# One sum, reciprocal and widening per unit in a top-k attention kernel with a maxout layer

## The chip, the cores and the metric

The kernel runs on one core of a Trainium2 chip. The metric is the device time of one execution in microseconds (us), as the median of three runs. One further execution was recorded by the hardware profiler; all rows below come from it. In the rows PE is the engine of the matrix products, PEld its weight loads, DVE the vector engine, ACT the engine that applies functions, POOL the general one, SP the one that issues transfers.

## What is computed

Attention over 8 batches of 8 heads, 576 positions of 64 values each, where each query keeps its 32 largest scores. The result goes through three products whose element-wise maximum is taken, and one output product.

```python
def _attn_ref(q, k, v):
    scores = scale * np.matmul(q, k.transpose(0, 1, 3, 2))
    kth = np.partition(scores, -top_k, axis=-1)[..., -top_k:-top_k + 1]
    scores = np.where(scores >= kth, scores, -1000000000.0)
    scores = scores - np.max(scores, axis=-1, keepdims=True)
    attn = np.exp(scores)
    attn = attn / (np.sum(attn, axis=-1, keepdims=True) + 1e-09)
    return np.matmul(attn, v)

def _moe_ref(x, w1, w2, w3, w_out):
    h = np.maximum(np.maximum(x @ w1, x @ w2), x @ w3)
    return h @ w_out
```

## The kernel before

**Units and groups.** Attention is cut into 80 units. 64 of them take two groups of 128 queries of one pair of heads, 16 are half units with one group (the last 64 queries of two pairs of heads). A group has two tiles of 128 rows by 576 scores, one for each head; `ssb` holds the scores.

**The steps of a unit.** `qk` (line 458, PE) makes the scores and `evac` (501, ACT) moves them out. `sweep` (510, DVE) takes maxima of seven parts of each row; `negate` and `pivot` (516 to 542) make of them a first guess at the 32nd largest. `sign` (550, ACT), `window` (555, POOL), `below` (559, DVE) and `pick` (570 to 575) find the exact value, and `mask` (598, DVE) pushes out the scores under it. `expo` (607, ACT) takes the exponential and the row sums. Then, group by group, `denominator` (615, ACT) adds 1e-9 to the two sums, `inverse` (622, DVE) takes the reciprocals, and `widen` (627, ACT) spreads the reciprocal of each head over 64 columns as `rsw`. `turn` (PE) transposes: pieces T(g,0) and T(g,1) are four 128x128 blocks each of the group's two tiles (658), and T(g,2) is one more block of the scores (653) and the widened reciprocals (655). `turned` (666, ACT) copies each of the three out of PSUM to `pT`. `values` (683, PE) multiplies by v; `scaled_x` (700, DVE) multiplies by the reciprocals; `high_x` (703, ACT) and `low_x` (707, POOL) split the result into two halves of 16 bits.

**The layer behind it.** The three products (`layer`, 740, PE), the maximum (747 on ACT, 749 on DVE), the split (752 on ACT, 755 on POOL) and the output product (`layer2`, 801, PE; 807 on ACT) are called the fill. A batch has a first part of 256 positions and a second of 320, and a part may start when the units of its positions are done. The weights come as raw words that DVE decodes (263 to 265), and ACT (309, 312) and POOL (315) cut into two halves, all inside the first 220 us: casts 1 to 18 at line 312 belong to the first products, six for each third of the columns, casts 19 to 24 to the output product.

**What sets the order.** Every step is a `Piece` with an engine, a cost and a rank: the number of its unit plus a shift from the table `OFFSETS`. `in_order` goes through a planned time and gives each engine its pieces one after the other; fill pieces go in between when nothing of higher rank can start. On PE a piece of qk is in mode "rows", one of `values` in "columns", all else in none; `STICK` says how much later a piece of the present mode may be and still be taken. The result is one fixed order for each engine; on the chip each engine goes through its own and waits where an operand isn't there yet. `rings` holds the number of buffers for each tile.

Of the kernel before, what the change touches and what calls it, by code (L numbers as in the profile page):

```python
# [33 lines left out]
AHEAD_OF_FILL = 6  # L34
STICK = 220.8
WINDOW = 150
# [105 lines left out]
PACE = 0.9  # L142
SAVED_IN = 2600.0
FIRST = ((0, 1),)
# [6 lines left out]
SCORES = 960  # L151
PATIENCE = {'PE': 137.2, 'DVE': 138.1, 'ACT': 0.0, 'POOL': 1.4, 'SP': 0.0}


@with_exitstack
def kernel(ctx, tc, q, k, v, moe_w1, moe_w2, moe_w3, moe_w_out, out):
    nc = tc.nc
# [139 lines left out]
    def cut(j, part):  # L297
# [16 lines left out]
        def low():  # L314
# [4 lines left out]
    rings = {nm: Ring(k) for nm, k in dict(s=2, tr=2, m=2, ssb=NSSB, L=NSM, nA=NSM, n8=NSM, nb=3, w=NWB, oh=2, pm=PMB, rs=3, sums=3, den=3,  # L319
                                           rsw=2, pT=1, xs=2, junk=2, early=2, stage=2, books=2, vt=6, x=2, h1=3, ob=2, ws=2, qk=3).items()}  # L320

# [114 lines left out]
    def open_unit(n):  # L436
        b, hps, us = units[n]
        if b not in books:
            books[b] = (wk.tile([P, NT, NW], F32, name="Q"), wk.tile([P, NT], F32, name="kth"), wk.tile([P, NT], F32, name="lost"))
        nt = tiles_of(n)  # L440
        i0 = hps[0] * 2 * NU + 2 * us[0] if us[0] < NU else NP * 2 * NU + hps[0]
        Q, kth, lost = books[b]
        st[n] = dict(nt=nt, ssb=[], s={}, w={}, rsw={}, Q=Q[:, i0:i0 + nt], kth=kth[:, i0:i0 + nt], lost=lost[:, i0:i0 + nt])

# [172 lines left out]
    def inverse(n, g):  # L617
        d = st[n]
        if g == 0:
            d["rs"] = sm.tile([P, 4], F32, name="rs", bufs=3)  # L620
        ts = slice(2 * g, 2 * g + 2)
        nc.vector.reciprocal(d["rs"][:, ts], d["den"][:, ts])
# [36 lines left out]

    def turned(n, g, i):  # L660
        d = st[n]
        if (g, i) == (0, 0):
            d["pT"] = wk.tile([P, 2, 10, P], F32, name="pT", bufs=1)
        pt, pT = d.pop(("pt", g, i)), d["pT"][:, g].rearrange("p i n -> p (i n)")
        m = 512 if i < 2 else 2 * P
        nc.scalar.copy(pT[:, 512 * i:512 * i + m] if i < 2 else pT[:, 8 * P:10 * P], pt[:, :m])  # L666

    def values(n):
# [5 lines left out]
        for x, hp in enumerate(hps):  # L674
            vt = v_of[b, hp]
            for i in range(5):
                for h in range(2):
                    block = 4 * h + i if i < 4 else 8
                    if us[0] < NU:
                        to, keys = xp[64 * h:64 * h + 64, :P * len(us)], d["pT"][:, 0:len(us), block, :]  # L680
                    else:
                        to, keys = xp[64 * h:64 * h + 64, 64 * x:64 * x + 64], d["pT"][:, 0, block, 64 * x:64 * x + 64]
                    nc.tensor.matmul(to, vt[:, block if i < 4 else 8 + h, :], keys, start=(i == 0), stop=(i == 4))  # L683
# [11 lines left out]
    def scaled_x(n):  # L695
        b, hps, us = units[n]
        d = st[n]
        xs = d["xs"] = sm.tile([P, 2 * P], F32, name="xs", bufs=2)
        x, xp = (t[:, :P * len(us)].rearrange("p (t n) -> p t n", n=P) for t in (xs, d["xp"]))
        nc.vector.scalar_tensor_tensor(x, xp, vs_of[b][0], d["pT"][:, 0:len(us), 9, :], ALU.mult, ALU.mult)  # L700

# [170 lines left out]
    def attention(n):  # L872
# [61 lines left out]
        last_x[:] = [d["x", nt - 1]]  # L934
        held(n, "nb").extend(d["x", t] for t in range(nt))
        for g in gs:
            xs = [d["x", 2 * g], d["x", 2 * g + 1]]
            p(("d", g), "ACT", 130, lambda g=g: denominator(n, g), needs=xs + ([d["d", 0]] if g else []), takes=[] if g else [("den", held(n, "den"))])
            p(("r", g), "DVE", 72, lambda g=g: inverse(n, g), needs=[d["d", g]] + ([d["r", 0]] if g else []), takes=[] if g else [("rs", held(n, "rs"))])
            p(("z", g), "ACT", 280, lambda g=g: widen(n, g), needs=[d["r", g]], takes=[("rsw", held(n, "rsw", g))])  # L940
            held(n, "den").append(d["r", g])
            held(n, "sums").append(d["d", g])
            held(n, "rs").append(d["z", g])
            for i in range(3):
                rel = []
                p(("T", g, i), "PE", 470 if i < 2 else 240, lambda g=g, i=i: turn(n, g, i),
                  needs=[xs[i]] + last_v if i < 2 else [*xs, d["z", g], *last_v], takes=[("tr", rel)])
                p(("E", g, i), "ACT", 478 if i < 2 else 264, lambda g=g, i=i: turned(n, g, i),
                  needs=[d["T", g, i]] + ([] if (g, i) == (0, 0) else [d["E", 0, 0]]), takes=[("pT", held(n, "pT"))] if (g, i) == (0, 0) else [])
                rel.append(d["E", g, i])  # L950
                held(n, "pm", g).append(d["T", g, i])
            held(n, "rsw", g).append(d["T", g, 2])
        m = len(us) * P
# [131 lines left out]
    with tc.If(redo != 0):  # L1085
        with tc.For_i(0, B, 1) as b:
# [6 lines left out]
            for A in range(0, NP, 2):  # L1093
                for hp in (A, A + 1):
                    load_qk(B, hp)
                for x in [(B, (hp,), (u,)) for hp in (A, A + 1) for u in range(NU)] + [(B, (A, A + 1), (NU,))]:
# [6 lines left out]
                    for t in range(2):  # L1103
                        mask(i, t)
                        expo(i, t)
                    denominator(i, 0)
                    inverse(i, 0)
                    widen(i, 0)
                    for t in range(3):
# [56 lines left out]
```

## Time and profile before

| | |
|---|---|
| median of 3 runs | 1206.98 us (1206.4 to 1207.8) |
| profiled execution, own time | 1208.61 us |
| profiled execution, span from first to last instruction | 1206.8 us |
| busy share of the span: PE, DVE, ACT, POOL | 93%, 90%, 85%, 46% |
| mean granted clock of PE | 0.961 of full speed |
| chain that ended last: PE, DVE, ACT, POOL | 54%, 17%, 6%, 2% of the span |

The busy share is an average over three stages. In the first some 200 us PE works with gaps and at a clock that is granted in part, while the weights are decoded beside the first units. From there to about 1110 us PE and DVE are both nearly always busy. In the last 90 us DVE and ACT fall off and PE goes on alone. Matmuls are pipelined and their ends are modelled, so a PE that the page shows as busy may still be held up between two of them.

### The profile page before, as it was taken

The numbers are of one execution on the slowest core, as the hardware profiler recorded it, in microseconds if no ns is written. First come the engines' busy times: TensorE is split into PE (matmuls) and PEld (weight loads), VectorE is DVE, ScalarE is ACT, GpSimd is POOL, SyncE is SP. The second block draws the span as 40 slices with busy tenths as digits, with TensorE's granted clock in tenths as the row PEclk, the third lists the DMA queues.
The fourth block names the chain that finished last, engine by engine and source line by source line (L and its number), as shares of the span: only waits on it lengthen the run. The fifth ranks groups of instructions, "written<-read, shape, count | busy, mean of one in ns | idle before, by whom it ended". The sixth has DMA issues, their size and how long they took to land.

```text
span 1206.8 us, 27344 instructions
## 1 busy us (share of the span) xinstructions
PE 1126.2 (93%) x8799; PEld 775.9 (64%) x8799; DVE 1087.3 (90%) x5376; ACT 1025.1 (85%) x2701; POOL 549.4 (46%) x503
## 2 busy tenths in 40 slices
PE   6458678999999999999999999999999999999997
PEld 3225545666776658667676758666676767666865
DVE  7999989999999989999999999999999999999310
ACT  6799899999979999898888989989989898897411
POOL 2353446555454455454543544445445444546110
PEclk8679768999999999999999999999999999999999
DMA  7244501101310102020301102020100101000000
GB/s 265 75 168 151 200 1 64 38 16 48 128 32 30 51 19 71 10 71 16 114 32 43 39 18 72 18 63 2 56 26 30 51 19 30 10 11 1 19 18 29
DMA packets 28631, 65.00 MB, mean 54 GB/s; under 512 B 3009, under 2 KB 3265, under 8 KB 28481
## 3 DMA queue, kind: packets, MB, share of 16 engines
q1 hardware_dynamic: 28176, 62.76, 15.5%
q8 instruction: 71, 1.16, 0.4%
q14 instruction: 80, 0.65, 0.2%
q10 hardware_dynamic: 304, 0.43, 0.1%
HBM read 49.02 MB, written 14.16 MB: 52 GB/s over the span
## 4 chain that ended last, share of the span: by engine, by line
PE 54%; DVE 17%; ACT 6%; POOL 2%; issue 2%; POOLq 0%; ACTq 0%; DVEq 0%
PE m L740 24%; PE m L801 8%; PE tr L683 7%; PE tr L658 7%; PE s L458 6%; DVE ssb L598 5%; DVE L L510 4%; DVE Q L559 3%; ACT pm L607 2%; POOL w L555 2%; ACT w L550 2%; DVE h L749 1%; ACT pT L666 1%; PE tr L653 1%; DVE nR L534 1%
## 5 line engine op out<-in xcount | busy, mean ns | idle before, releaser
L555 POOL TENSOR_TENSOR w<-ssb,w 128x576 f32<-128x576 f32 x288 | 402.2, 1416 | 280.3 <-ACT w L550 225.4
L740 PE MATMUL m<-xh,wall 128*128 128x256 f16 (+1 forms) x2304 | 435.2, 287 | 4.6 <-POOL wall L315 2.4
L740 PEld LDWEIGHTS <-wall 128*128 128x128 f16 x3456 | 336.8, 98 | 91.1 <-issue 10.5
L740 PE MATMUL m<-xl,wall 128*128 128x320 f16 (+1 forms) x1152 | 330.1, 287 | 0.0
L510 DVE MAX8 L<-ssb 128x8 f32<-128x82 f32 (+1 forms) x2016 | 312.5, 229 | 6.0 <-ACT ssb L501 6.0
L607 ACT ACTIVATE pm<-ssb,nb 128x576 f32<-128x576 f32 x288 | 223.3, 776 | 45.3 <-DVE ssb L598 44.7
L598 DVE SCALAR_TENSOR_TENSOR ssb<-ssb,kth 128x576 f32<-128x576 f32 x288 | 235.0, 847 | 2.2
L550 ACT ACTIVATE w<-ssb,Q 128x576 f32<-128x576 f32 x288 | 223.6, 777 | 10.4 <-DVE Q L542 9.3
L559 DVE MAX8 Q<-w 128x8 f32<-128x576 f32 x288 | 213.4, 750 | 16.6 <-POOL w L555 15.4
L666 ACT COPY pT<-tr 128x512 f32<-128x512 f32 (+1 forms) x432 | 217.8, 514 | 11.1 <-PE tr L655 7.2
L658 PE MATMUL tr<-ident,pm 128*128 128x128 f32 x1152 | 181.3, 285 | 22.2 <-ACT pm L607 11.5
L458 PE MATMUL s<-qk 64*128 64x288 f32 (+1 forms) x1216 | 179.5, 448 | 16.5 <-ACT ssb L501 11.3
L501 ACT ACTIVATE ssb<-s 128x576 f32<-128x576 f32 x272 | 175.6, 655 | 13.9 <-PE s L458 13.5
L683 PE MATMUL tr<-pT,vt 128*64 128x256 f32 (+1 forms) x1920 | 182.3, 339 | 4.0 <-ACT pT L666 3.8
L658 PEld LDWEIGHTS tr<-ident,pm 128*128 128x128 f32 x1152 | 132.5, 144 | 74.1 <-ACT pm L607 25.9
L683 PEld LDWEIGHTS tr<-pT,vt 128*64 128x64 f32 x1920 | 110.4, 140 | 74.2 <-issue 14.4
L755 POOL TENSOR_TENSOR hl<-h,hh 128x256 f16<-128x256 f32 (+1 forms) x96 | 70.9, 738 | 161.0 <-ACT hh L752 70.3
L458 PEld LDWEIGHTS s<-qk 64*128 64x128 f32 (+1 forms) x1216 | 93.9, 183 | 77.1 <-ACT ssb L501 29.8
L749 DVE SCALAR_TENSOR_TENSOR h<-m,h 128x256 f32<-128x256 f32 (+1 forms) x192 | 86.0, 448 | 53.6 <-PE m L740 52.8
L801 PE MATMUL m<-wall,hh 128*128 128x512 f16 (+1 forms) x444 | 129.0, 374 | 0.0
L707 POOL TENSOR_TENSOR xl<-xs,xh 128x256 f16<-128x256 f32 (+1 forms) x80 | 51.0, 638 | 149.7 <-DVE Q L542 30.3
L801 PE MATMUL m<-wall,hl 128*128 128x512 f16 (+1 forms) x222 | 82.9, 374 | 0.0
(96 smaller groups left out, 1098.5 us busy)
## 6 DMA issues: line engine op xcount, KB each, us to landing
vt<-in_v_dram SPq DMA_DIRECT2D x32, 320.0 KB, 3.0
qk<-in_k_dram SPq DMA_DIRECT2D x34, 288.0 KB, 3.2
qk<-in_q_dram SPq DMA_DIRECT2D x33, 288.0 KB, 3.6
wall<-in_moe_w_dram SPq DMA_DIRECT2D x16, 512.0 KB, 6.4
out_dram<-ob SPq DMA_DIRECT2D x32, 256.0 KB, 2.0
ssb<-saved SPq DMA_DIRECT2D x8, 576.0 KB, 3.7
saved<-xh SPq DMA_DIRECT2D x4, 576.0 KB, 2.9
saved<-xl SPq DMA_DIRECT2D x4, 576.0 KB, 3.2
```

The lines of the kernel that those rows point to most:

```text
L458: nc.tensor.matmul(to[:, h, :HALF], both[sl, 0, c0:c0 + m], both[sl, 1, i * HALF:(i + 1) * HALF], start=True, stop=True)
L510: nc.vector.max(d["L"][:, t, k, :], d["ssb"][t][:, EDGES[k]:EDGES[k + 1]])
L550: nc.scalar.activation(d["w"][t], d["ssb"][t], AF.Sign, bias=d["Q"][:, t, 0:1], scale=-1.0, accum_out=d["cnt"][:, t:t + 1])
L555: return nc.gpsimd.tensor_tensor(d["w"][t], d["ssb"][t], d["w"][t], ALU.mult)
L559: nc.vector.max(d["Q"][:, t, 1:NW], d["w"].pop(t))
L598: return nc.vector.scalar_tensor_tensor(ss, ss, d["kth"][:, t:t + 1], ss, ALU.is_lt, ALU.subtract, accum_out=d["lost"][:, t:t + 1])
L607: nc.scalar.activation(d["pm", t // 2][:, t % 2], d["ssb"][t], AF.Exp, bias=d["nb"][:, t:t + 1], scale=-1.0 / SHRINK, accum_out=d["sums"][ ...
L658: nc.tensor.transpose(pt[:, j * P:(j + 1) * P], pm[:, i, 64 * i + j * P:64 * i + (j + 1) * P], ident)
L666: nc.scalar.copy(pT[:, 512 * i:512 * i + m] if i < 2 else pT[:, 8 * P:10 * P], pt[:, :m])
L683: nc.tensor.matmul(to, vt[:, block if i < 4 else 8 + h, :], keys, start=(i == 0), stop=(i == 4))
L740: nc.tensor.matmul(box["ps", i][:, :c1 - c0], a, bb[:, kc, c0:c1], start=(kc == 0 and k == 0), stop=(kc == KC - 1 and k == 2))
L801: nc.tensor.matmul(box["po"][:n, :ds.stop - ds.start], a[:, f, cs], columns_of(bb, ds), start=(f == 0 and k == 0), stop=(f == FC - 1 and k ...
```

## The change

The sums, the reciprocals and the widening are done once per unit. `den`, `rs` and `rsw` hold up to four columns, two per group; `rsw` has one buffer in place of two. T(g,2) of a group that isn't the unit's last transposes its block of scores alone; that of the last group transposes its block and then one block of reciprocals for each group of the unit. `pT` is laid out anew: nine blocks per group, and the reciprocals of all groups behind them. The constants of the planner are other ones: the table `OFFSETS` in all its entries, `STICK`, `SAVED_IN` and `PATIENCE`.

```diff
-STICK = 220.8
+STICK = 1234.8
...
-OFFSETS = {'A': -26.65, 'C0': -66.87, 'C1': 27.6, 'C2': 14.16, 'C3': 24.81, ...
+OFFSETS = {'A': -40.54, 'C0': -79.36, 'C1': 25.16, 'C2': 15.17, 'C3': 25.57, ...
...
-SAVED_IN = 2600.0
+SAVED_IN = 1800.0
...
-PATIENCE = {'PE': 137.2, 'DVE': 138.1, 'ACT': 0.0, 'POOL': 1.4, 'SP': 0.0}
+PATIENCE = {'PE': 175.8, 'DVE': 111.3, 'ACT': 0.0, 'POOL': 0.0, 'SP': 0.0}
...
-                                           rsw=2, pT=1, xs=2, ...
+                                           rsw=1, pT=1, xs=2, ...
...
-    def denominator(n, g):
-        d = st[n]
-        if g == 0:
-            d["den"] = sm.tile([P, 4], F32, name="den", bufs=3)
-        ts = slice(2 * g, 2 * g + 2)
-        nc.scalar.activation(d["den"][:, ts], d["sums"][:, ts], AF.Copy, bias=1e-9)
+    def denominator(n):
+        d = st[n]
+        d["den"] = sm.tile([P, 4], F32, name="den", bufs=3)
+        nc.scalar.activation(d["den"][:, :d["nt"]], d["sums"][:, :d["nt"]], AF.Copy, bias=1e-9)
...
-    def widen(n, g):
-        d = st[n]
-        rsw = d["rsw"][g] = sm.tile([P, 2, D], F32, name="rsw", bufs=2)
-        nc.scalar.copy(rsw, d["rs"][:, 2 * g:2 * g + 2].unsqueeze(2).to_broadcast((P, 2, D)))
+    def widen(n):
+        d = st[n]
+        nt = d["nt"]
+        d["rsw"] = sm.tile([P, 4, D], F32, name="rsw", bufs=1)
+        nc.scalar.copy(d["rsw"][:, :nt], d["rs"][:, :nt].unsqueeze(2).to_broadcast((P, nt, D)))
...
             nc.tensor.transpose(pt[:, :P], pm.rearrange("p t s -> p (t s)")[:, 4 * P:5 * P], ident)
-
-            nc.tensor.transpose(pt[:, P:2 * P], d["rsw"].pop(g).rearrange("p h d -> p (h d)"), ident)
+            if 2 * g + 2 == d["nt"]:
+                rsw = d["rsw"].rearrange("p t d -> p (t d)")
+                for k in range(g + 1):
+                    nc.tensor.transpose(pt[:, (1 + k) * P:(2 + k) * P], rsw[:, k * P:(k + 1) * P], ident)
             return
...
-        m = 512 if i < 2 else 2 * P
+        m = 512 if i < 2 else P if 2 * g + 2 < d["nt"] else (2 + g) * P
...
-            p(("d", g), "ACT", 130, lambda g=g: denominator(n, g), needs=xs + ([d["d", 0]] if g else []), ...
-            p(("r", g), "DVE", 72, lambda g=g: inverse(n, g), needs=[d["d", g]] + ([d["r", 0]] if g else []), ...
-            p(("z", g), "ACT", 280, lambda g=g: widen(n, g), needs=[d["r", g]], takes=[("rsw", held(n, "rsw", g))])
+        p("d", "ACT", 104 + 13 * nt, lambda: denominator(n), needs=[d["x", t] for t in range(nt)], ...
+        p("r", "DVE", 75, lambda: inverse(n), needs=[d["d"]], takes=[("rs", held(n, "rs"))])
+        p("z", "ACT", 91 + 55 * nt, lambda: widen(n), needs=[d["r"]], takes=[("rsw", held(n, "rsw"))])
```

Three places show how the order moves. The first is PE about 100 us into the program, where one two-group unit of the first batch is transposed (`ident,pm` are blocks of the scores, `ident,rsw` the reciprocals, `s<-qk` new scores); before:

```order
L458 MATMUL s<-qk 128x288 x4
L653 MATMUL tr<-ident,pm 128x128
L655 MATMUL tr<-ident,rsw 128x128
L658 MATMUL tr<-ident,pm 128x128 x4
L458 MATMUL s<-qk 128x288 x4
```

and now:

```order
L458 MATMUL s<-qk 128x288 x4
L650 MATMUL tr<-ident,pm 128x128
L657 MATMUL tr<-ident,pm 128x128 x4
L458 MATMUL s<-qk 128x288 x8
L650 MATMUL tr<-ident,pm 128x128
L654 MATMUL tr<-ident,rsw 128x128 x2
L657 MATMUL tr<-ident,pm 128x128 x4
```

The reciprocals of the first group have moved behind the scores of the second; the four blocks of T(1,1) stand behind the two of the reciprocals.

The second is ACT at the weights of the second third of the columns (`ws` and the cast to `wall` are the two steps of one cut, `w,cnt` the signs of a search, `pT<-tr` copies of transposed blocks); before:

```order
L550 ACTIVATE w,cnt<-ssb,Q 128x576 x5
L666 COPY pT<-tr 128x512
L309 ACTIVATE ws<-wall,down_w_1648 128x512 x2
L312 CAST wall<-ws 128x2x256 x2
L516 ACTIVATE nA<-L 128x112
L666 COPY pT<-tr 128x512
L627 COPY rsw<-rs 128x128 x2
```

and now:

```order
L550 ACTIVATE w,cnt<-ssb,Q 128x576
L312 CAST wall<-ws 128x2x256
L309 ACTIVATE ws<-wall,down_w_1576 128x512
L516 ACTIVATE nA<-L 128x112
L312 CAST wall<-ws 128x2x256
L607 ACTIVATE pm,sums<-ssb,nb 128x576
L666 COPY pT<-tr 128x512
L613 ACTIVATE den<-sums 128x4
```

The cuts have moved ahead of signs and copies. Counted through ACT's order, there stand ahead of the 18th cast now 4 signs, 2 copies of 512 columns, 1 move of scores and 1 square fewer than before, and 8 sums and 8 widenings fewer.

The third is PE at the last `values` of the program (the two rows `tr<-pT,vt`); before:

```order
L740 MATMUL m<-xl,wall 128x256
L683 MATMUL tr<-pT,vt_89 64x64 x10
L683 MATMUL tr<-pT,vt_90 64x64 x10
L740 LDWEIGHTS wall
L740 MATMUL m<-xh,wall 128x256
```

and now:

```order
L807 MATMUL m<-wall,hl 128x512
L689 MATMUL tr<-pT,vt_89 64x64 x10
L689 MATMUL tr<-pT,vt_90 64x64 x10
L807 LDWEIGHTS hh
L807 MATMUL m<-wall,hh 128x512
```

The last values have moved ahead of fill. Before, 174 products of 256 columns of the last batch's first part stood behind them; now 15 output products of the batch before and all 216 of that part do. Behind both stands the same rest: 36 output products, 216 products of 320 columns, and the last output products. In the part of the program that is run PE changes its mode 346 times in place of 330.

## Rows read from the trace of the kernel before

**Rows 1.** Section 1 of the page: busy us, share of the span, instructions of each engine.

```profile
PE 1126.2 (93%) x8799; PEld 775.9 (64%) x8799; DVE 1087.3 (90%) x5376; ACT 1025.1 (85%) x2701; POOL 549.4 (46%) x503
```

**Rows 2.** Stretches of 30 us: start:end, length, busy (instructions) of each engine, PEclk, DMA.

```profile
150.00:180.00 30.00, 22.54 (x120) 13.22 (x118) 25.83 (x85) 27.00 (x66) 14.49 (x13) 0.64 0.00 1
180.00:210.00 30.00, 24.21 (x202) 16.83 (x199) 27.68 (x127) 28.13 (x69) 17.78 (x17) 0.89 0.20 65
210.00:240.00 30.00, 28.70 (x203) 19.13 (x202) 29.68 (x154) 28.68 (x76) 16.51 (x16) 1.00 0.11 39
...
1140.00:1170.00 30.00, 30.00 (x223) 21.60 (x221) 5.57 (x15) 5.58 (x13) 3.47 (x5) 1.00 0.05 19
```

**Rows 3.** Chain that ended last, in order of time: start us, us, what.

```profile
1096.98 1.47 DVE ssb L598 x4
1100.44 1.24 PE tr L658 x8
...
1131.21 1.31 PE tr L683 x40
...
1134.70 17.03 PE m L740 x156
1151.73 7.77 PE m L801 x36
1159.50 29.34 PE m L740 x216
```

**Rows 4.** Groups by form: count, busy us, mean ns, idle before and its releasers.

```profile
L666 ACT COPY pT<-tr 128x512 f32<-128x512 f32 x288 | 166.7, 582 | 3.5 <-PE tr L658 2.3 <-ACT h L747 0.3
...
L666 ACT COPY pT<-tr 128x256 f32<-128x256 f32 x144 | 53.3, 378 | 7.6 <-PE tr L655 7.2
...
L627 ACT COPY rsw<-rs 128x128 f32<-128x128 f32 x144 | 43.2, 305 | 3.3 <-DVE rs L622 2.6
...
L615 ACT ACTIVATE den<-sums 128x2 f32<-128x2 f32 x144 | 29.6, 205 | 0.5
...
L622 DVE RECIPROCAL rs<-den 128x2 f32<-128x2 f32 x144 | 22.2, 154 | 5.6 <-ACT den L615 5.6
```

**Rows 5.** ACT in order of time: start us, us, instruction.

```profile
573.10 0.20 ACT L615 ACTIVATE den<-sums 128x2 f32<-128x2 f32 x1
573.21 0.76 ACT L607 ACTIVATE pm<-ssb,nb 128x576 f32<-128x576 f32 x1
...
573.97 0.28 ACT L627 COPY rsw<-rs 128x128 f32<-128x128 f32 x1
574.15 0.77 ACT L607 ACTIVATE pm<-ssb,nb 128x576 f32<-128x576 f32 x1
```

**Rows 6.** DVE in order of time, where attention ends.

```profile
1119.00 0.81 DVE L598 SCALAR_TENSOR_TENSOR ssb<-ssb,kth 128x576 f32<-128x576 f32 x1
...
1119.74 0.16 DVE L622 RECIPROCAL rs<-den 128x2 f32<-128x2 f32 x1
1119.81 0.48 DVE L635 TENSOR_TENSOR junk<-Q,kth 128x324 f32<-128x324 f32 x1
```

**Rows 7.** PE in order of time, where it goes from products to scores.

```profile
568.09 0.30 PE L740 MATMUL m<-xl,wall 128*128 128x320 f16 x1
568.32 1.24 PE L458 MATMUL s<-qk 64*128 64x288 f32 x8
```

**Rows 8.** POOL and PE in order of time, near 200 us.

```profile
198.72 1.15 POOL L315 TENSOR_TENSOR wall<-ws,wall 128x512 f16<-128x512 f32 x1
...
199.81 0.40 PE L740 MATMUL m<-xh,wall 128*128 128x256 f16 x2
```

**Rows 9.** Waits between 210 and 1115 us: us in total, times, longest.

```profile
DVE Q L559 <- POOL w L555: 12.5, 20, 1.7
...
PEld tr L658 <- ACT pm L607: 14.1, 34, 0.8
...
PEld tr L655 <- ACT rsw L627: 1.2, 5, 0.4
```

More of the change, by code (lines that the diff above doesn't have):

```diff
@@ L319 @@
     rings = {nm: Ring(k) for nm, k in dict(s=2, tr=2, m=2, ssb=NSSB, L=NSM, nA=NSM, n8=NSM, nb=3, w=NWB, oh=2, pm=PMB, rs=3, sums=3, den=3,
-                                           rsw=2, pT=1, xs=2, junk=2, early=2, stage=2, books=2, vt=6, x=2, h1=3, ob=2, ws=2, qk=3).items()}
+                                           rsw=1, pT=1, xs=2, junk=2, early=2, stage=2, books=2, vt=6, x=2, h1=3, ob=2, ws=2, qk=3).items()}
     def piece(engine, cost, run, needs=(), rank=(0.0, None), takes=(), mode=None, alone=False):
@@ L442, in open_unit @@
         Q, kth, lost = books[b]
-        st[n] = dict(nt=nt, ssb=[], s={}, w={}, rsw={}, Q=Q[:, i0:i0 + nt], kth=kth[:, i0:i0 + nt], lost=lost[:, i0:i0 + nt])
+        st[n] = dict(nt=nt, ssb=[], s={}, w={}, Q=Q[:, i0:i0 + nt], kth=kth[:, i0:i0 + nt], lost=lost[:, i0:i0 + nt])
     def qk(n, g, i):
@@ L662, in turned, with keys_of, shares_of @@
         if (g, i) == (0, 0):
-            d["pT"] = wk.tile([P, 2, 10, P], F32, name="pT", bufs=1)
-        pt, pT = d.pop(("pt", g, i)), d["pT"][:, g].rearrange("p i n -> p (i n)")
-        m = 512 if i < 2 else 2 * P
-        nc.scalar.copy(pT[:, 512 * i:512 * i + m] if i < 2 else pT[:, 8 * P:10 * P], pt[:, :m])
+            d["pT"] = wk.tile([P, 20, P], F32, name="pT", bufs=1)
+        pt, pT = d.pop(("pt", g, i)), d["pT"].rearrange("p i n -> p (i n)")
+        m = 512 if i < 2 else P if 2 * g + 2 < d["nt"] else (2 + g) * P
+        to = 9 * P * g + 512 * i
+        nc.scalar.copy(pT[:, to:to + m], pt[:, :m])
+    def keys_of(d, ng, block):
+        return d["pT"][:, :18].rearrange("p (g i) n -> p g i n", g=2)[:, 0:ng, block, :]
+    def shares_of(d, ng):
+        return d["pT"][:, 9 * ng:10 * ng]
     def values(n):
@@ L679, in values @@
                     if us[0] < NU:
-                        to, keys = xp[64 * h:64 * h + 64, :P * len(us)], d["pT"][:, 0:len(us), block, :]
+                        to, keys = xp[64 * h:64 * h + 64, :P * len(us)], keys_of(d, len(us), block)
                     else:
-                        to, keys = xp[64 * h:64 * h + 64, 64 * x:64 * x + 64], d["pT"][:, 0, block, 64 * x:64 * x + 64]
+                        to, keys = xp[64 * h:64 * h + 64, 64 * x:64 * x + 64], keys_of(d, 1, block)[:, 0, 64 * x:64 * x + 64]
                     nc.tensor.matmul(to, vt[:, block if i < 4 else 8 + h, :], keys, start=(i == 0), stop=(i == 4))
@@ L935, in attention @@
         held(n, "nb").extend(d["x", t] for t in range(nt))
+        last_g = gs[-1]
+        p("d", "ACT", 104 + 13 * nt, lambda: denominator(n), needs=[d["x", t] for t in range(nt)], takes=[("den", held(n, "den"))])
+        p("r", "DVE", 75, lambda: inverse(n), needs=[d["d"]], takes=[("rs", held(n, "rs"))])
+        p("z", "ACT", 91 + 55 * nt, lambda: widen(n), needs=[d["r"]], takes=[("rsw", held(n, "rsw"))])
+        held(n, "den").append(d["r"])
+        held(n, "sums").append(d["d"])
+        held(n, "rs").append(d["z"])
         for g in gs:
             xs = [d["x", 2 * g], d["x", 2 * g + 1]]
-            p(("d", g), "ACT", 130, lambda g=g: denominator(n, g), needs=xs + ([d["d", 0]] if g else []), takes=[] if g else [("den", held(n, "den"))])
-            p(("r", g), "DVE", 72, lambda g=g: inverse(n, g), needs=[d["d", g]] + ([d["r", 0]] if g else []), takes=[] if g else [("rs", held(n, "rs"))])
-            p(("z", g), "ACT", 280, lambda g=g: widen(n, g), needs=[d["r", g]], takes=[("rsw", held(n, "rsw", g))])
-            held(n, "den").append(d["r", g])
-            held(n, "sums").append(d["d", g])
-            held(n, "rs").append(d["z", g])
             for i in range(3):
                 rel = []
-                p(("T", g, i), "PE", 470 if i < 2 else 240, lambda g=g, i=i: turn(n, g, i),
-                  needs=[xs[i]] + last_v if i < 2 else [*xs, d["z", g], *last_v], takes=[("tr", rel)])
-                p(("E", g, i), "ACT", 478 if i < 2 else 264, lambda g=g, i=i: turned(n, g, i),
+                final = g == last_g
+                p(("T", g, i), "PE", 470 if i < 2 else 122 if not final else 122 * (2 + g), lambda g=g, i=i: turn(n, g, i),
+                  needs=[xs[i]] + last_v if i < 2 else [*xs, *([d["z"]] if final else []), *last_v], takes=[("tr", rel)])
+                p(("E", g, i), "ACT", 478 if i < 2 else 155 if not final else 155 + 109 * (1 + g), lambda g=g, i=i: turned(n, g, i),
                   needs=[d["T", g, i]] + ([] if (g, i) == (0, 0) else [d["E", 0, 0]]), takes=[("pT", held(n, "pT"))] if (g, i) == (0, 0) else [])
@@ L951, in attention @@
                 held(n, "pm", g).append(d["T", g, i])
-            held(n, "rsw", g).append(d["T", g, 2])
+        held(n, "rsw").append(d["T", last_g, 2])
         m = len(us) * P
@@ L1105 @@
                         expo(i, t)
-                    denominator(i, 0)
-                    inverse(i, 0)
-                    widen(i, 0)
+                    denominator(i)
+                    inverse(i)
+                    widen(i)
                     for t in range(3):
```

12 lines of the change are left out of this document (5 added, 7 removed).

## The prediction

> **What bounds the kernel now.** I read the busy shares first [rows 1]: PE 93% and DVE 90%, too close together to name one. So I went on to the stretches of 30 us [rows 2]. They show three stages. [...] From 210 us on the clock is full, PE is busy 28.7 of 30 and DVE 29.7. In the last 90 us DVE is at 5.6 of 30 and PE at 30.
>
> The chain of waits [rows 3] tells which of the two engines counts at the end: it leaves DVE for the last time at about 1100 us, behind masks that start at 1096.98, and from 1100.44 until the last product is out it is PE alone. DVE has finished its last mask at 1119.8 [rows 6], but the last values start only at 1131.2 [rows 3]. Between them lie an exponential (0.76), a sum (0.20), a reciprocal (0.16), a widening (0.30), transposes and copies of 0.4 to 0.6, which I put at some 5 us [rows 4 to 6]. So PE is about 6 us late there, with fill still to do. The end is set by PE: its work, and the time that it could not use.
>
> **The change part by part.** *ACT's instructions.* 64 units lose one sum and have one wide widening for two narrow ones. By mean durations [rows 4] a sum is 205 ns. Copies of 512 and 256 columns take 582 and 378 ns, so 0.80 ns a column, and a widening of 256 takes 305 + 128 x 0.80 = 407 in place of 610: together 0.408 us a unit, 26 us. But ACT's instructions overlap: behind a sum the next one starts after 0.11 us, behind a widening after 0.18 [rows 5]. Counted from start to start a unit saves 0.11 + (2 x 0.18 - 0.28) = 0.19 us, in all 12 us of ACT's 1025. I take 12. The copies out of PSUM are 128 + 384 columns in place of 256 + 256, which is the same sum.
>
> *DVE's reciprocals.* 64 fewer; the next instruction starts 0.07 us behind one [rows 6], so 4.5 us (9.9 at their mean of 154 ns [rows 4]). DVE's last mask comes some 5 us earlier, at 1115.
>
> *PE's transposes.* Their number is the same: 1 + 3 in place of 2 + 2. Nothing is saved on the engine that sets the end.
>
> *PE's modes.* PE changes its mode 16 times more. A product of 320 columns is followed by the next after 0.136 us (29.34 us for 216 [rows 3]), but by scores after 0.23 [rows 7]: a change costs 0.09 us, so +1.4 us. This is PE's own time, in a stage where it is full, and I count it whole.
>
> *The last values.* Behind them stand now 42 more products of 256 columns and 15 more output products. By the chain [rows 3] these are 42 x 0.109 (17.03 us for 156) + 15 x 0.216 (7.77 for 36) = 7.8 us. Ahead of them stands as much less. Attention thus runs ahead of the fill by about what DVE saves (5 us) and a part of what PE was late (6 us). For the end this is nothing in itself: PE does the same work in another order. Without the 5 us of DVE and the lateness as a cover it would cost up to 7.8.
>
> *The cuts of the weights.* This is the only place where PE has much time to win. Ahead of the 18th cast ACT has 8 sums and 8 widenings fewer (8 x 0.19 = 1.5 us), 4 signs (each as wide as an exponential, 4 x 0.76 [rows 5]), 2 copies of 512 columns (2 x 0.5 from start to start), a move of scores and a square (some 1.3), together about 7 us. ACT is busy 27 to 28 of 30 us there [rows 2], so the products of the last third of the columns may start near 193 us in place of 199.8 [rows 8]. How much of it stays: the output products behind them need casts 19 to 24, which stand no earlier in ACT's work; and DVE, which paces attention, comes to the same place after the same work. Bounds 0 and -7; I take the middle, -3.5.
>
> *PE held up in the middle.* The trace doesn't show what 12 us less on ACT do to it. What stands in its records: weight loads for transposes that wait for the exponential, 14.1 us in 34 waits, and DVE behind POOL's windows, 12.5 us [rows 9], which wait for ACT's signs. One end is 0, the other a half of the 14.1. A lighter ACT (1% of its work) shortens queues only a little: I take -1.5. A gain of more is not excluded, and neither is a loss, since all of the order is new: the constants moved in every entry, and so did the chance with which an engine finds its operand ready. I put that at 4 us to either side.
>
> *SP's transfers.* One pair of loads of queries and keys goes ahead of four loads of weights, and reloads of saved scores stand a few places on. No row of before shows an engine held by SP behind the first scores; I cost it at nothing, and it would cost as much as DVE's first decodes came late.
>
> The sum: +1.4 - 3.5 - 1.5 = -3.6 us, on a span of 1206.8 us. The profiled execution took 1208.6 with what lies around the span, 1.6 above the median; I take the difference from the median, 1206.98, and get 1203.4.
>
> **The rivals.** *A, no change.* PE's work is the same and both engines are full; what the cuts win at 190 us is lost until 260 us, since attention is paced by DVE, and the modes cost 1.4. Then 1206.98 + 1.4 - 1.5 = 1206.9. For it speaks that DVE is at 29.7 of 30 right behind the start [rows 2]. Against it: PE was late at the end, so DVE's time isn't the whole account.
>
> *B, slower: PE waits for the widened reciprocals.* The two blocks of reciprocals now wait for four exponentials, one sum, one reciprocal and a widening that is 0.1 us longer, and the last four blocks of the unit stand behind them. Before, such waits came to 1.2 us in 5 in the middle [rows 9], 0.24 us each. Should every second of the 64 units pay twice that, the price is 32 x 0.48 = 15 us; at every fourth 7.7, and 1203.4 + 7.7 = 1211.1. It decides from about 13 such units on, where 6 us are lost and the result is slower. Against it: PE's order puts fill ahead of these blocks in most units, and the first group's wait is gone. [...]
>
> *C, more gain.* The 7 us of the cuts stay whole and ACT's relief takes half of the 14.1: 1206.98 + 1.4 - 7 - 7 = 1194.4; with half of either part more than I took, 1198.
>
> *D, the change doesn't do what it says.* The order shows fewer sums, reciprocals and widenings, so I leave it out.
>
> **How the numbers follow.** About 0.2% (2.4 us) is what a measurement of this kernel can tell from no change. The forecast, 1203.4 (from 1199 to 1204.5): 0.36. C, under 1199: 0.12. A, from 1204.6 to 1209.4: 0.30. B, over that: 0.22. So faster 0.48, same 0.30, slower 0.22. The range goes from 1195 (C's end left out) to 1212 (B with every fourth unit).
>
> **What would show it.** In the trace of the changed kernel: POOL's piece behind the 18th cast near 192 us and PE with fewer gaps between 180 and 215 us (right), or PE with new gaps between 215 and 260 (A). DVE's last mask near 1113 and the last values within 8 us behind it; 80 reciprocals and 80 widenings, the wide ones near 407 ns. ACT's busy time down by about 12 us or, summed without overlap, more. B would show as waits of PE's weight loads for the widening well over 1.2 us between 210 and 1115 us. The prediction is wrong if the stretch from 210 to 1100 us holds PE up by over 5 us more or less than before, which the new order could do without any of the named parts.

## The result and the profile after

The changed kernel takes 1218.19 us (median of 3, 1216.6 to 1218.51), 1.0089 of the kernel before [1.0066, 1.0112]: slower by 11 us where 3.6 us less were forecast, and outside the range. The profiled execution took 1218.19 us, its span is 1216.4, 9.6 us more than before.

The page's busy times, to be held against [rows 1]: ACT has lost 9.6 us and 128 instructions, as the change intends, DVE 64 instructions, and DVE is busy 3.4 us *longer*.

```profile
PE 1133.7 (93%) x8799; PEld 775.1 (64%) x8799; DVE 1090.7 (90%) x5312; ACT 1015.5 (83%) x2573; POOL 550.9 (45%) x503
```

The stretches of [rows 2] in the changed kernel:

```profile
150.00:180.00 30.00, 19.04 (x118) 11.07 (x118) 27.71 (x78) 27.30 (x66) 17.19 (x14) 0.76 0.06 23
180.00:210.00 30.00, 25.99 (x218) 19.39 (x220) 28.12 (x144) 27.92 (x70) 17.80 (x17) 0.89 0.32 104
210.00:240.00 30.00, 28.63 (x199) 18.56 (x196) 29.34 (x134) 28.43 (x71) 17.73 (x16) 1.00 0.12 39
...
1140.00:1170.00 30.00, 30.00 (x240) 23.29 (x238) 5.72 (x16) 5.72 (x13) 4.02 (x6) 1.00 0.03 10
```

The start is no worse: 218 products in place of 202 from 180 to 210 us. The loss lies behind it. One long stretch from 210 to 1110 us, first of the kernel before, then of the changed one:

```profile
210.00:1110.00 900.00, 893.71 (x7212) 624.68 (x7212) 871.30 (x4476) 818.90 (x2203) 444.07 (x402) 1.00 0.12 39
```

```profile
210.00:1110.00 900.00, 891.16 (x7124) 614.14 (x7120) 870.20 (x4393) 808.33 (x2084) 440.22 (x398) 1.00 0.12 39
```

PE is shown as busy alike, but has got 88 fewer products done, 60 of them of 320 columns: some 11 us of work by the distances given below. The chain that ended last shows where they stand now (start us, us, what; against [rows 3]):

```profile
1133.10 1.31 PE tr L689 x40
1134.41 3.34 PE m L807 x15
1137.76 1.31 PE m L746 x12
1139.18 22.27 PE m L746 x204
1161.45 7.77 PE m L807 x36
1169.22 29.34 PE m L746 x216
```

Behind the last values stand 15 output products and 12 + 204 products of 256 columns, ahead of the rest that both orders share. This is as the order had said (42 products and 15 output products more than before): from the start of those values to the end of the span it is 83.4 us in place of 75.7. The values themselves come 1.9 us later (1133.1 for 1131.2), and DVE's last mask ends at 1124.0 in place of 1119.8. In all, 1.9 + 7.7 = 9.6 us.

The page also says that the chain has changed sides. Before, it ran through PE for 54% of the span and through DVE for 17%; now:

```profile
DVE 43%; PE 36%; ACT 11%; POOL 6%; issue 4%; DMA 0%; POOLq 0%; DVEq 0%; ACTq 0%
```

For what follows I measure **PE's lost time**: from each product's start to the next one's, less the distance that its kind keeps in an unbroken row (0.109, 0.136 or 0.216 us for products of 256, 320 and 512 columns, 0.109 for a transposed block, 0.1075 and 0.121 for whole values and scores), less 0.093 per change of mode (scores start 0.229 us behind a product of 320 columns, where another product starts after 0.136). From 210 to 1140 us it is 36.1 us before and 46.5 now. With 16 x 0.093 = 1.5 more for modes and 2.4 less lost ahead of 210 us (108.9, now 106.5) that is 9.5 us, the whole difference.

### The profile page after: what moved, and what is told of

It is laid out like the page before. It is cut to its first block, busy times and chain, and to the rows that moved or that the text cites. A ratio compares the mean times of both kernels' runs of the same rounds, so it can differ in the third digit from the quotient of the medians.

```text
span 1216.4 us, 27195 instructions
## 1 busy us (share of the span) xinstructions
PE 1133.7 (93%) x8799; PEld 775.1 (64%) x8799; DVE 1090.7 (90%) x5312; ACT 1015.5 (83%) x2573; POOL 550.9 (45%) x503
## 4 chain that ended last, share of the span: by engine, by line
DVE 43%; PE 36%; ACT 11%; POOL 6%; issue 4%; DMA 0%; POOLq 0%; DVEq 0%; ACTq 0%
PE m L746 16%; DVE L L510 11%; DVE ssb L598 10%; DVE Q L559 7%; PE tr L689 5%; PE m L807 5%; POOL w L555 5%; PE tr L657 4%; PE s L458 4%; ACT pm L607 3%; DVE h L755 3%; ACT w L550 2%; DVE nR L534 2%; ACT pT L666 2%; DVE n L536 1%
## 5 line engine op out<-in xcount | busy, mean ns | idle before, releaser
L598 DVE SCALAR_TENSOR_TENSOR ssb<-ssb,kth 128x576 f32<-128x576 f32 x288 | 239.9, 860 | 2.5
L550 ACT ACTIVATE w<-ssb,Q 128x576 f32<-128x576 f32 x288 | 224.2, 779 | 19.0 <-DVE Q L542 11.9
L666 ACT COPY pT<-tr 128x512 f32<-128x512 f32 (+3 forms) x432 | 216.6, 514 | 12.3 <-PE tr L657 8.7
L458 PE MATMUL s<-qk 64*128 64x288 f32 (+1 forms) x1216 | 179.7, 450 | 18.1 <-ACT ssb L501 12.9
L458 PEld LDWEIGHTS s<-qk 64*128 64x128 f32 (+1 forms) x1216 | 94.3, 183 | 75.1 <-ACT ssb L501 27.7
L807 PE MATMUL m<-wall,hl 128*128 128x512 f16 (+1 forms) x222 | 82.9, 373 | 0.0
```

Source lines behind the costliest of these rows:

```text
L458: nc.tensor.matmul(to[:, h, :HALF], both[sl, 0, c0:c0 + m], both[sl, 1, i * HALF:(i + 1) * HALF], start=True, stop=True)
L550: nc.scalar.activation(d["w"][t], d["ssb"][t], AF.Sign, bias=d["Q"][:, t, 0:1], scale=-1.0, accum_out=d["cnt"][:, t:t + 1])
L598: return nc.vector.scalar_tensor_tensor(ss, ss, d["kth"][:, t:t + 1], ss, ALU.is_lt, ALU.subtract, accum_out=d["lost"][:, t:t + 1])
L666: nc.scalar.copy(pT[:, to:to + m], pt[:, :m])
L807: nc.tensor.matmul(box["po"][:n, :ds.stop - ds.start], a[:, f, cs], columns_of(bb, ds), start=(f == 0 and k == 0), stop=(f == FC - 1 and k ...
```

## The experiments

Each row is a profiled run, except for the medians. The ratios are to runs of the kernel before that were taken beside each kernel (medians of 1206.96 to 1208.18 us). "For pT": waits of transposes' weight loads for copies out of PSUM (`turned`), 210 to 1115 us. The last two columns run from the end of the last mask to the start of the last values, and from there to the end of the span.

| kernel | median us | ratio to before | PE lost 210-1140 | for pT | last mask | to values | behind |
|---|---|---|---|---|---|---|---|
| before | 1206.98 | | 36.1 | 5.3 | 1119.8 | 11.3 | 75.7 |
| changed | 1218.19 | 1.0089 [1.0066, 1.0112] | 46.5 | 16.4 | 1124.0 | 9.0 | 83.4 |
| e1 merge, old numbers | 1227.31 | 1.0166 [1.0149, 1.0183] | 43.2 | 9.2 | 1124.9 | 14.2 | 85.3 |
| e2 split, new numbers | 1308.54 | 1.0838 [1.0820, 1.0856] | 131.6 | 23.8 | 1225.6 | 9.7 | 72.9 |
| e3 changed + 160 reciprocals | 1232.95 | 1.0213 [1.0196, 1.0230] | 60.4 | 21.9 | 1138.9 | 9.3 | 83.1 |
| e7 changed - 80 reciprocals | 1213.70 | 1.0053 [1.0036, 1.0070] | 44.2 | 15.2 | 1120.1 | 9.0 | 82.9 |
| e4 before + 144 reciprocals | 1211.07 | 1.0039 [1.0023, 1.0054] | 38.7 | 6.1 | 1121.8 | 11.3 | 75.8 |
| e5 merge, old order | 1205.89 | 0.9988 [0.9979, 0.9997] | 34.6 | 4.7 | 1117.5 | 11.3 | 75.7 |
| e6 split, new order | 1221.40 | 1.0120 [1.0105, 1.0136] | 50.6 | 19.8 | 1127.4 | 9.0 | 83.5 |
| e8 fill 9 us earlier | 1370.21 | 1.1354 [1.1337, 1.1372] | 161.2 | 47.0 | 1279.1 | 13.8 | 75.1 |
| e10 block moved back | 1246.96 | 1.0321 [1.0306, 1.0335] | 74.8 | 46.8 | 1152.1 | 10.5 | 83.0 |
| e11 block moved up | 1250.17 | 1.0347 [1.0333, 1.0361] | 76.9 | 46.4 | 1162.7 | 11.8 | 76.0 |
| e12 fill 1.5 us earlier | 1249.15 | 1.0341 [1.0327, 1.0355] | 72.6 | 7.1 | 1159.7 | 12.1 | 74.9 |
| e13 block behind two fills | 1227.33 | 1.0168 [1.0154, 1.0182] | 56.8 | 31.3 | 1134.1 | 10.2 | 83.0 |
| e14 block behind one fill | 1222.42 | 1.0121 [1.0106, 1.0137] | 51.2 | 22.7 | 1128.4 | 9.8 | 83.2 |

**Half of the change each (e1, e2).** First the code with the planner's old constants, then the old code with the new ones.

```diff
 # e1: the changed kernel with before's STICK, OFFSETS, SAVED_IN, PATIENCE
 # e2: the kernel before with the changed kernel's
+OFFSETS = {... 'd0': -1.56, 'd1': -1.56, 'r0': 2.35, 'r1': 2.35, 'z0': 0.15, 'z1': 0.15, ...}
```

> The merged code with the planner's constants of the kernel before (for the sum, the reciprocal and the widening, those of the second group). In its order 36 pieces of six products and 8 output pieces stand behind the last values, against 29 and none before: 9.8 us more of PE's work. Theory 1 (DVE paces attention from 300 us on, the merge makes the plan run attention ahead of what DVE gives, and the fill that is left over stands behind the end of attention): slower than before by 5 to 12 us, 1212 to 1219. Theory 2 (the merge is harmless, the new constants made an order in which PE waits more): 1202 to 1207.

> The code of before, two sums, reciprocals and widenings a unit, with the planner's constants of the changed kernel (both groups get the unit's). Behind the last values stand 25 pieces of six products, 4 fewer than before (2.6 us). Theory 1: within 3 us of before, 1204 to 1210. Theory 2: as slow as the changed kernel or slower, 1215 to 1222.

Both missed, 1227 and 1309 us. Ahead of 210 us e1 loses 12 us more than the changed kernel (10 more than before), and it has 85.3 us left behind the last values; in e2 PE's transposes wait for exponentials for 50.7 us, where before they waited 14.1. With either half replaced the planner makes another order altogether, so these two don't tell code and order apart. They show that constants fit one set of pieces and costs.

**DVE made heavier or lighter (e3, e7, e4).** e7 leaves the division by the sums out.

```diff
 # e3, in inverse(n)                       # e4, the same once per group, in the kernel before
+        more = sm.tile([P, 4], F32, name="more", bufs=3)
+        for _ in range(2):
+            nc.vector.reciprocal(more[:, :d["nt"]], d["den"][:, :d["nt"]])
 # e7, in inverse(n)
-        d["rs"] = sm.tile([P, 4], F32, name="rs", bufs=3)
-        nc.vector.reciprocal(d["rs"][:, :d["nt"]], d["den"][:, :d["nt"]])
+        d["rs"] = d["den"]
```

> The changed kernel with two more reciprocals a unit, written to a tile that nobody reads, 160 in all at 0.07 us from start to start: 11 us more on DVE, the order else the same. Theory 1: the end moves by nearly all of it, 1227 to 1230. Theory 2 (PE's own waits and order set the end): by less than 4 us, up to 1222.

> The changed kernel without its 80 reciprocals (the widening takes the sums, so the output is multiplied by them in place of divided): 7 us less on DVE and one step less between exponential and widened block, the order else the same. Theory 1: 5 to 7 us less than the changed kernel, 1211 to 1213. Theory 2: 1216 to 1218.

> The kernel before with one more reciprocal behind each of its 144, into a tile that nobody reads: by the run of the changed kernel with 160 more (16.7 us of DVE's busy time) about 15 us more on DVE. Theory 1 (DVE paces this kernel too, nearly one to one, and PE was not really late): 1207 + 13 to 15 = 1220 to 1222 us. Rival (the reading of the prediction: PE is some 6 us late behind DVE's last mask, so the first 6 us of DVE's time are free): 1207 + 15 - 6 = 1216, from 1214 to 1218.

Busy times on the page, of e3, then of e4:

```profile
PE 1138.5 (92%) x8799; PEld 773.5 (63%) x8799; DVE 1107.4 (90%) x5472; ACT 1019.5 (83%) x2573; POOL 551.6 (45%) x503
```

```profile
PE 1123.8 (93%) x8799; PEld 772.6 (64%) x8799; DVE 1093.6 (90%) x5520; ACT 1026.3 (85%) x2701; POOL 549.5 (45%) x503
```

e3 gives DVE 16.7 us more and ends 14.8 us later; e7 takes 4 us from it and ends 4.5 earlier. Both times miss theory 1's ranges, by 3.0 us (e3's reciprocals cost 16.7 us and not 11) and by 0.7, and are further from theory 2's. In the changed kernel DVE's time comes out at the end nearly one to one. e4 missed in both expectations, since its 144 reciprocals cost DVE only 6.3 us (0.044 each; in e3, where two in a row write one tile, 0.104), of which 4.2 went into time in which DVE had been idle. The last mask came 2.0 us later, and so did the end of the span (2.1; the median 3.8, against 1207.3 for before beside it). In the old order only a part of DVE's added time comes out. The table's last two columns settle the other question: whatever is done to DVE, the distance from the last mask to the last values keeps to 11.3 us in the old order and 9.0 to 9.3 in the new one. It is no time that PE is late by and that could cover something; it belongs to the order.

**Merge and order apart (e5, e6).** The plan of one kernel is kept piece by piece, and only what the pieces issue is changed.

```diff
 # e5: the kernel before; d, r and z of a first group issue nothing
     def denominator(n, g):
-        if g == 0: ...
-        ts = slice(2 * g, 2 * g + 2)
+        if 2 * g + 2 < d["nt"]:
+            return
...
 # e6: the changed kernel; d, r and z issue two narrow instructions
+        for t in range(0, d["nt"], 2):
+            nc.vector.reciprocal(d["rs"][:, t:t + 2], d["den"][:, t:t + 2])
```

> The merge alone: before's plan is kept piece by piece, so every engine has before's order; the first group's sum, reciprocal and widening fall away, the second group's do both, T(0,2) is one block and T(1,2) three. PE has before's 330 mode changes and before's 67.8 us of products behind the last values. Theory 1 (the loss lies in the order that was redone with it; the merge itself takes 4.5 us of reciprocals from DVE and gives most of it to the end): 1202 to 1205 us. Rival 2 (the merge itself costs: the two blocks of reciprocals wait for four exponentials, and PE or DVE wait behind them): 1210 to 1219, with PE's weight loads waiting for the widening well over the 1.2 us that before had. If it is between, 1206 to 1208, the merge is worth nothing and costs nothing.

> The changed kernel in its own order, but with each sum, reciprocal and widening done as two, one right behind the other (64 more of each: by the records some 12 us more on ACT, 4.5 on DVE; the transposes stay as they are). Theory 1 (the order set the loss, the merge is worth what DVE saves): 4 to 5 us over the changed kernel, 1222 to 1224 us, so that order and merge add up (before 1207, +11 the order and more, -4.5 the merge). Rival 2 (the merge itself costs, by its later reciprocals): this kernel waits as late and comes out no better, but a split costs nothing either: 1218 to 1219.

These two decide. The merge in the old order is worth 1.4 us (0.9988 [0.9979, 0.9997], against 1207.3 for before beside it). The split in the new one costs 3.2, less surely so, since the intervals of the two ratios, 1.0105 to 1.0136 and 1.0066 to 1.0112, overlap. Both effects are smaller than theory 1 had them: 1205.9 lies between its range and that of no effect, 1221.4 just under its range, and rival 2's ranges are further off. So the merge does what it says and gains a little; from e5 to the changed kernel the instructions are the same, and the order alone costs 1218.2 - 1205.9 = 12.3 us (11.9 by the spans). e5 is also the fastest of all kernels here. Its busy times:

```profile
PE 1124.6 (93%) x8799; PEld 775.3 (64%) x8799; DVE 1084.3 (90%) x5312; ACT 1014.9 (84%) x2573; POOL 549.3 (46%) x503
```

ACT is 10.2 us lighter than before, DVE 3.0, and the last mask and the end of the span come 2.3 us earlier. At most those 2.3 us came of ACT's 10.2; how they divide between the two isn't shown (at e4's rate, 2.1 for 6.3, DVE's 3.0 would give 1.0).

What the order does to PE is seen in the waits of its weight loads, of the kernel with the old order (e5), then of the changed one (us in total, times, longest):

```profile
PEld tr L663 <- ACT pm L607: 12.9, 32, 0.9
...
PEld tr L663 <- ACT pT L672: 3.8, 11, 0.7
PEld tr L660 <- ACT rsw L630: 2.3, 8, 0.5
PEld tr L656 <- ACT pT L672: 0.9, 3, 0.4
```

```profile
PEld tr L657 <- ACT pm L607: 13.8, 38, 0.8
PEld tr L657 <- ACT pT L666: 10.7, 31, 0.5
PEld tr L650 <- ACT pT L666: 5.7, 17, 0.8
PEld tr L650 <- ACT pm L607: 4.7, 9, 1.2
...
PEld tr L654 <- ACT rsw L624: 2.8, 8, 0.6
```

The transposes wait 18.5 us for the exponentials (`pm`) in place of 12.9, and 16.4 us for the copies (`pT`) of those before them in place of 4.7: two buffers of PSUM (`tr`) serve three pieces per group, and the third needs the first one's copy. For the widened reciprocals (`rsw`) they wait 2.7 us in e5 and 3.2 in the changed kernel. Ahead of single blocks T(g,2) PE loses 1.6 us before and 8.7 now, 7.0 of it at those of first groups. In before's order 29 units have T(0,0) T(0,1) T(1,0) T(1,1) and then both single blocks; in the new one 30 have T(0,0) T(0,2) T(0,1): freed from the widening, the block was put forward.

**Fill against attention (e8, e12).** Every fill piece is issued earlier by a part of its planned time.

```diff
+    rest = sorted(plan, key=lambda x: x.start - (SHIFT if id(x) in fill else 0.0))
 # e8: the changed kernel's plan, SHIFT = 9000 ns; e12: e5's plan, SHIFT = 1500 ns
```

> The changed kernel, with the same plan, but every piece of the fill (products, maxima, splits, output products) is issued 9 us of planned time earlier against attention's pieces; the order inside each of the two stays. Behind the last values stand 67.8 us of products, as in the kernel before, in place of 75.6; PE changes its mode 368 times in place of 346 (22 x 0.09 = 2.0 us). Theory 1a (the new order let attention run ahead of the fill, so PE waits for DVE in the middle and has the fill left at the end): 1218.2 - 7.8 + 2.0 = 1212.4, from 1210 to 1214 us, with the last values at about 1133 as in the changed kernel. Rival 3 (DVE sets the pace, and fill put earlier puts its maxima earlier too and moves the last mask and the last values back by as much): 1218 to 1222, with the last values some 8 us later.

> The merge in before's order, with every piece of the fill issued 1.5 us of planned time earlier against attention (where 9 us in the changed kernel's plan had made 1370). 328 mode changes in place of 330, 67.2 us behind the last values in place of 67.8. If the end follows from the last mask and what stands behind it: 1205 to 1206 us. If harm grows evenly with the shift (150 us for 9): 1205.9 + 25 = 1231. In between, over 1208, the fill's maxima then stand on DVE ahead of their products.

In e8 DVE stands before maxima whose products aren't there and before windows that come late (210 to 1250 us; in the changed kernel, from 210 to 1115, these waits are 0.6 and 14.2 us):

```profile
DVE h L797 <- PE m L788: 54.5, 37, 5.8
...
DVE Q L601 <- POOL w L597: 37.2, 50, 2.2
```

75.1 us are left behind the last values, as wanted, and the last mask comes 155 us later. None of the expectations came near. Even 1.5 us of shift cost 43 us, so harm does not grow evenly either. The two runs say nothing on the 7.7 us; they show how narrow the fit of a plan is.

**The single block (e10, e11, e13, e14).** Only T(0,2) and its copy move: behind T(1,0) in the changed kernel (e10), behind T(0,1) in e5's order (e11), and in the changed kernel behind the second or first fill product that follows (e13, e14).

```diff
+        d["T", 0, 2].after, d["E", 0, 2].after = d["T", 1, 0], d["E", 1, 0]     # e10
+        d["T", 0, 2].after, d["E", 0, 2].after = d["T", 0, 1], d["E", 0, 1]     # e11
+                x.start = later[-1].start + 0.001                                # e13, e14
```

> The changed kernel and its plan, with one step of it put elsewhere: the first group's single block T(0,2) and its copy go behind the first transposes of the second group, T(1,0), in place of between or right behind the first group's own. Nothing else moves (DVE, POOL and SP keep their order up to two entries, PE has the same 346 mode changes and 75.6 us behind the last values). In the trace of the changed kernel PE loses 8.2 us from 210 to 1140 us ahead of single blocks, 7.0 of it at 56 of the first group's, in place of 1.5 in the kernel before, where that block stood later. Theory 4 (the change freed that block from the widening, the new plan puts it forward, and there it waits for a copy or the second exponential): PE's lost time falls by 5 to 7 us and the end comes at 1211 to 1214 us. Rival 1 (DVE sets the pace; the wait only goes on to the next transposes): 1216.5 to 1219.

> The other way round: the merge in before's order (1205.9 us), with the first group's single block and its copy put right behind its own T(0,1), as far forward as the changed kernel mostly has it. Nothing else moves (DVE, POOL and SP as they were, 330 mode changes, 67.8 us behind the last values). Theory 4: PE loses some 5 us more ahead of single blocks, and the end comes at 1209 to 1213 us. Rival 1: 1205 to 1207.

> The changed kernel and its plan, with the first group's single block and its copy put two fill products further back, so that it seldom stands right behind four-block transposes: 11 times in the order in place of 29 (in both kernels with the block moved, e10 and e11, it stood so 66 and 71 times, and PE lost 19 us in that place against 2.9 in the changed kernel and 0.1 in the kernel before). 346 mode changes and 75.6 us behind the last values stay. Theory 5 (a single block right behind transposes finds both buffers of PSUM taken, and this standing is a part of what the new order costs): PE's lost time ahead of single blocks falls from 7.3 to some 3 us, the end comes at 1213 to 1216 us. Rival 1 (DVE sets the pace): 1217 to 1219. Rival 6 (any step moved out of a fitted plan costs, whatever it is moved to): over 1222.

> The same with one fill product in place of two: the block stands right behind transposes 12 times, ACT's order has 57 entries changed in place of 145, DVE's 24 in place of 4. Theory 5: 1213 to 1216 us. Rival 1: 1217 to 1219. Rival 6: over 1220.

PE in e11, in order of time, at one such block (L702 are the two four-block pieces, L695 is the single one, L791 a product of the fill):

```profile
699.51 1.09 PE L702 MATMUL tr<-ident,pm 128*128 128x128 f32 x8
701.60 0.33 PE L695 MATMUL tr<-ident,pm 128*128 128x128 f32 x1 [1.00 <-ACT pT L711]
701.77 0.43 PE L791 MATMUL m<-xh,wall 128*128 128x320 f16 x2
```

PE stands for 1.00 us until the copy of the first of the three is out, and no product passes the block: the one at 701.77 starts right behind it. Put right behind transposes (66 and 71 times, against 29 in the changed kernel and 16 in e5), these blocks alone lose 19 us of PE in e10 and 20 in e11, and the whole kernels 29 and 44. The waits of these blocks in e11 (L695), and of the four-block pieces (L702):

```profile
PEld tr L702 <- ACT pT L711: 24.9, 22, 2.4
...
PEld tr L695 <- ACT pT L711: 21.5, 31, 1.4
```

So e10 and e11 show what the block costs PE right behind transposes. Theory 4 isn't borne out: e11's loss has its direction, at many times its size, and e10, where it had 6 us to gain, is slower too. e13 and e14 took the block from behind the transposes (11 and 12 times), and PE's loss there fell from 2.9 us to 0.0 and 0.1, as theory 5 has it. But the transposes that follow now wait, the loss from one block to the next of the four-block pieces going from 8.1 us to 14.7 and 10.6, and both kernels are slower than the one they started from, by 9.1 and 4.2 us. Rival 6 holds: all six plans that I moved by hand (e8, e10 to e14) lost against the plan they came from. The wait for a free buffer isn't one step's; it passes to the next.

## Why the prediction was wrong

**What it had right.** PE's 16 mode changes (346 for 330), 80 reciprocals and 80 widenings, and their prices: the wide widening takes 408 ns (407 worked out), and 64 fewer reciprocals save DVE 4.5 us from start to start.

```profile
L624 ACT COPY rsw<-rs 128x256 f32<-128x256 f32 x64 | 26.1, 408 | 2.5 <-DVE rs L618 2.2
...
L613 ACT ACTIVATE den<-sums 128x4 f32<-128x4 f32 x64 | 13.2, 207 | 0.3
L618 DVE RECIPROCAL rs<-den 128x4 f32<-128x4 f32 x64 | 10.6, 166 | 0.5 <-ACT den L613 0.5
```

The cuts came as forecast: POOL's piece behind the 18th cast starts at 191.39 us, in place of 198.72 [rows 8], PE loses 2.4 us less ahead of 210 us (-3.5 taken), and from 210 to 240 us it is as busy as before (28.63 for 28.70), so rival A's reason is refuted. Ahead of 210 us the first products wait for POOL's cuts for 2.0 us (4 waits), in place of 5.3 (3 waits).

```profile
191.39 1.39 POOL L315 TENSOR_TENSOR wall<-ws,wall 128x512 f16<-128x512 f32 x1 [2.31 <-ACT wall L312]
```

**The term that failed** is "PE held up in the middle", -1.5 with 4 to either side: +10.4 us. It was sized from what a lighter ACT does to the waits that stood in the records, and e5 shows -1.5 us of lost time (its DVE is lighter too, so it may be luck that the term came out). The new order itself had no term but those 4 us. Its price is 12.3 us; what this consists of is told under "What stays open". Of PE's waits the one that grew most, transposes waiting for copies, stood at 5.3 us before and was not among those read.

**"The last values ... nothing in itself"** rested on two covers that weren't there. DVE's 5 us: the last mask came 4.2 us later, not 5 earlier. And "PE is about 6 us late" behind the last mask: e3 to e7 show that distance to be fixed by the order, and never used up. The 7.8 us, priced as the cost without cover, came out as 7.7; the new order took 2.3 off the distance itself (9.0 for 11.3), so that 5.4 are left. In PE's account this is the same loss as the middle's: work that PE didn't do there is done at the end.

**DVE's last mask** was put at 1115 us by the prediction's sum and at 1113 in its list of signs, and ended at 1124.0. The 4.5 us of reciprocals were saved, and the masks took 4.9 back. By their group, before and now (288 each):

```profile
L598 DVE SCALAR_TENSOR_TENSOR ssb<-ssb,kth 128x576 f32<-128x576 f32 x288 | 235.0, 847 | 2.2
```

```profile
L598 DVE SCALAR_TENSOR_TENSOR ssb<-ssb,kth 128x576 f32<-128x576 f32 x288 | 239.9, 860 | 2.5
```

This is the order too: in e5 they take 234.9. Why is told in the last section.

**The rivals.** B named the right sign and 1211, with the wrong wait: for the widened reciprocals PE waits 3.2 us now and 1.2 before. e5, which waits 2.7 us for them and isn't slower than before, bears that out. A and C are refuted. What the prediction called a sign of error, over 5 us more in the middle, is what happened.

**What stays open.** Between e5 and the changed kernel, two orders of the same instructions, the table's last columns give the 12 us in two parts: the last mask comes 6.5 us later, and 5.4 us more lie behind it (9.0 + 83.4 for 11.3 + 75.7). The later mask is DVE's own work. Up to it DVE is busy 1075.6 us for e5's 1069.6, and idle 48.4 for 47.9. All its waits for PE from 210 to 1115 us in the changed kernel are these:

```profile
DVE xs L706 <- PE tr L689: 1.4, 2, 1.2
DVE h L755 <- PE m L746: 0.6, 1, 0.6
```

Of the 6.0 us the masks are 4 to 5, as the last section tells; the rest is spread over small steps. So PE's waits for copies grew by 11 us, but that they cost the changed kernel its time is not shown, and DVE's account speaks against it. They are shown to cost PE where the block was moved (e10, e11). Which pieces of the order put the masks beside POOL and the fill behind the last values stays open: no single move won any of it back. A third buffer for the transposes wasn't tried, nor an order with the masks kept off POOL's instructions.

## What to carry to other kernels

An edit that comes with a new order is two changes: replay the old order with the new code first, and the new order with the old code. Here the edit was worth 1.4 us and the order cost 12. In a fitted static order no term of a sum may stand for "the rest of the order": its bounds are those by which other orders of the same work differ, here 4 to 150 us, not a share of the waits on record. Time between two engines' last steps is cover only where a run has shown it to shrink.

## What the runs showed of the hardware

Of a mask on DVE and an instruction on POOL that overlapped, the one that started second took longer: a mask 1.24 us for 0.81, a window 1.83 us for 1.41. DVE and POOL in the changed kernel, in order of time:

```profile
625.27 1.24 DVE L598 SCALAR_TENSOR_TENSOR ssb<-ssb,kth 128x576 f32<-128x576 f32 x1
```

```profile
624.47 1.42 POOL L555 TENSOR_TENSOR w<-ssb,w 128x576 f32<-128x576 f32 x1 [0.76 <-ACT pm L607]
```

The mask overlaps the window for 0.62 us and takes 1.24 us for 0.81, which is what masks without such overlap take in each kernel. The 0.43 us added are the overlap less 0.2. So it was in all 84 masks of the kernel before, e5 and the changed kernel that start inside one instruction of POOL, overlap it for over 0.25 us and meet no other: the added time is the overlap less 0.19 to 0.20 us. The overlap of all masks sums to 17.0 us before, 17.3 in e5 and 26.6 in the changed kernel, and what they take over 0.81 us each to 9.4, 9.2 and 13.3 us. Where the mask came first, it took its usual time and the window was the longer one, 1.83 us for 1.41 (the kernel before):

```profile
155.14 0.82 DVE L598 SCALAR_TENSOR_TENSOR ssb<-ssb,kth 128x576 f32<-128x576 f32 x1
155.40 1.83 POOL L555 TENSOR_TENSOR w<-ssb,w 128x576 f32<-128x576 f32 x1 [1.52 <-DVE ssb L598]
```

These are the times; why the second of the two takes longer, no run shows.
